# Two attention layers of a decode step on one core: second attentions paired with the next token's first, FFNs of two tokens joined, half-size load buffers

## The chip, the core and the metric

The kernel runs on one core of one Trainium2 chip. The metric is the time on the device in microseconds (us), from repeated executions; lower is better.

Names used below: PE is TensorE (matmuls; every matmul is preceded by a weight load of its own), DVE is VectorE, ACT is ScalarE, SP is the engine whose queue issues all loads. "The queue" is this load queue. A load can be issued only when its buffer is free, so the queue itself can wait for PE or DVE.

## The reference

Four tokens (batch 4, one position each) go through attention, FFN, attention, FFN, and both layers use the same weights and the same caches.

```python
B, Sq, D = 4, 1, 448
Hq, Hkv, Sk, Dh = 16, 8, 8192, 256          # F = 1792 in the FFN
W = min(4096, max(256, Sk // 4))            # = 2048: only the last 2048 positions are attended

x = A_x
x = x + A(layernorm(x))     # q = x @ wq; softmax(q k^T / 16) v; @ wo
x = x + F(layernorm(x))     # (silu(x @ w_gate) * (x @ w_up)) @ w_down
x = x + A(layernorm(x))     # the same k_cache, v_cache, wq, wo
x = x + F(layernorm(x))
```

For one token and one of the 8 KV heads, K is 2048 x 256 bf16, which is 1 MiB, and V is 1 MiB too. That unit of work, (token, layer, KV head), is called a *pair* below; there are 4 x 2 x 8 = 64 of them. A *first* attention is layer 0, a *second* attention is layer 1. A second attention needs the same K and V as the first; what was kept on the chip isn't loaded again.

## The kernel before

Operations are put into a graph; a list scheduler with assumed durations fixes the order on each engine, and waits are placed after that. So on each engine the order is static: an operation that is ready waits behind one that is not. The parts that the change touches:

```python
NK = 2; NKT = 5; NV = 6            # raw K buffers, transposed K, V buffers: 1 MiB each
KEEP_KT = 4; KEEP_V = 4; FILL = 4  # heads kept from the first attention for the second

def pair_sequence():
    # ... one(t): 8 first pairs of token t; two(t): 8 second pairs, the kept heads first
    return (a + b[:FILL] + a2 + b[FILL:] + c[:FILL] + b2 + c[FILL:] + d[:FILL]
            + c2[:HKV - FILL] + d[FILL:] + c2[HKV - FILL:] + d2)
...
# all weights first: wq, then wo head by head, and the FFN's weights at rank 7.2
for nm, wsb, src in (("wg", wg_sb, B_w_gate), ("wu", wu_sb, B_w_up)):
    load(7.2, 3 * 458752, ...)
...
for pos, (t, layer, kvh) in enumerate(seq):
    # K: one load of 1 MiB into Kr, then two DVE transposes into KT          (L520, L526)
    # V: one load of 1 MiB into Vs                                           (L533)
    # scores: 32 matmuls, KT is the weight operand, q moves 8 columns        (L541)
    # max over positions by two matmuls M, exp on ACT, sums and a permutation on PE
    # p.V: 32 matmuls, V is the weight operand, p moves 2 columns            (L589)
    # out projection: 16 matmuls, wo is the weight operand, 1 column         (L608)
    ...
    def out_proj(e, p_=p_, t=t, kvh=kvh):
        for cc in range(4):
            for k in range(4):
                last = e.matmul(Ab[:, 4 * t + cc:4 * t + cc + 1], lhsT=wo_sb[:, 4 * kvh + k, c0:c0 + 128],
                                rhs=oT[p_][:, k // 2, k % 2:k % 2 + 1], ...)
    ...
    if all 8 heads of (t, layer) are done:       # written out in the kernel
        after_attention(t, pos)                  # residual, norm, ffn of this token alone: 168 matmuls
        if layer == 0: norm(t, pos); qproj([t], pos)
        else: store(t, pos)
```

## Time and profile before

| | before |
|---|---|
| median of the first three runs, us | 406.53 (403.88 to 406.92) |
| span of the profiled execution, us | 401.2 |
| loaded, MB | 112.83 |
| PE busy, us | 255.0 (64%) |
| DVE busy, us | 204.6 (51%) |

Lines of the profile page of the kernel before: the span, the busy time of each engine, then rows of 40 equal slices of the span (each digit is the busy share in tenths, GB/s is what the loads moved in a slice), the load queue's line of the queue table (packets, MB, share), and the chain of waits that ended last, by engine.

```profile
span 401.2 us, 16386 instructions
PE 255.0 (64%) x7572; PEld 231.9 (58%) x7572; DVE 204.6 (51%) x642; ACT 59.5 (15%) x302; POOL 2.7 (1%) x11
PE   2255005667777657877676766676776776677965
DMA  7999999968983999759839999379939969617200
GB/s 302 407 387 383 398 402 402 402 230 270 381 301 116 382 402 395 289 182 343 321 107 309 397 396 373 108 221 377 311 99 384 389 226 344 227 66 218 103 3 2
q1 hardware_dynamic: 39968, 112.83, 76.2%
PE 37%; DMA 19%; DVE 18%; SPq 12%; issue 10%; ACT 3%; DVEq 0%
```

No engine is full, and the loads aren't either: the DMA row swings between 9 and 3. The fifth and sixth digit of the PE row are 0: there PE waits for the first K, whose load stands behind the FFN's weights.

The table of windows of the kernel before: stretch, its length, busy time and instructions of each engine, granted clock, share of the DMA engines, GB/s.

```profile
core 0: us, PE busy (x) PEld busy (x) DVE busy (x) ACT busy (x) POOL busy (x), PEclk, DMA share, GB/s
50.00:80.00 30.00, 11.63 (x324) 10.12 (x324) 12.77 (x24) 2.60 (x14) 0.00 (x0) 1.00 1.04 403
100.00:355.00 255.00, 180.49 (x5524) 165.49 (x5521) 137.00 (x416) 40.21 (x212) 0.00 (x0) 1.00 0.80 293
335.80:375.90 40.10, 30.27 (x939) 28.09 (x940) 17.82 (x69) 5.57 (x28) 0.00 (x0) 1.00 0.59 207
375.90:401.20 25.30, 16.76 (x508) 15.24 (x505) 7.04 (x36) 3.08 (x18) 0.00 (x0) 1.00 0.01 3
```

The first line shows what the loads can do (403 GB/s), the second what they did (293).

The queue's waits in the kernel before (which load waited for which operation: total us, times, longest):

```profile
SPq L520 <- DVE KT L526: 92.0, 16, 10.2
SPq L533 <- PE Y L589: 51.6, 19, 7.5
SPq L520 <- DVE rs L578: 37.2, 6, 10.7
SPq L533 <- PE M L554: 32.5, 13, 5.1
```

L520 is the K load and L533 the V load. So loads stop because buffers are held: K waits for the transposes, V for the matmuls that read it.

### The profile page before, as it was taken

The numbers are of one execution on the slowest core, as the hardware profiler recorded it, in microseconds if no ns is written. First come the engines' busy times: TensorE is split into PE (matmuls) and PEld (weight loads), VectorE is DVE, ScalarE is ACT, GpSimd is POOL, SyncE is SP. The second block draws the span as 40 slices with busy tenths as digits, with TensorE's granted clock in tenths as the row PEclk, the third lists the DMA queues.
The fourth block names the chain that finished last, engine by engine and source line by source line (L and its number), as shares of the span: only waits on it lengthen the run. The fifth ranks groups of instructions, "written<-read, shape, count | busy, mean of one in ns | idle before, by whom it ended". The sixth has DMA issues, their size and how long they took to land.

```text
span 401.2 us, 16386 instructions
## 1 busy us (share of the span) xinstructions
PE 255.0 (64%) x7572; PEld 231.9 (58%) x7572; DVE 204.6 (51%) x642; ACT 59.5 (15%) x302; POOL 2.7 (1%) x11
## 2 busy tenths in 40 slices
PE   2255005667777657877676766676776776677965
PEld 2254004556676656766575665566765666667855
DVE  6721005688526635487336465286365665345432
ACT  1024001111012112111111111011121120111210
POOL 2000000000000000000000000000000000000000
DMA  7999999968983999759839999379939969617200
GB/s 302 407 387 383 398 402 402 402 230 270 381 301 116 382 402 395 289 182 343 321 107 309 397 396 373 108 221 377 311 99 384 389 226 344 227 66 218 103 3 2
DMA packets 40036, 113.88 MB, mean 284 GB/s; under 512 B 1816, under 2 KB 7968, under 8 KB 33440
## 3 DMA queue, kind: packets, MB, share of 16 engines
q1 hardware_dynamic: 39968, 112.83, 76.2%
q8 instruction: 59, 0.97, 1.0%
q14 instruction: 9, 0.07, 0.0%
HBM read 112.82 MB, written 0.00 MB: 281 GB/s over the span
## 4 chain that ended last, share of the span: by engine, by line
PE 37%; DMA 19%; DVE 18%; SPq 12%; issue 10%; ACT 3%; DVEq 0%
DMA Kr<-in_A_k_cache_dram 19%; DVE KT L526 11%; SPq L312 8%; PE Y L589 8%; PE S L541 7%; PE Z L437 6%; PE A L608 5%; PE Z L399 4%; SPq L533 3%; PE Z L456 3%; ACT oT L598 2%; PE Z L342 1%; ACT qb L421 1%; DVE negm L557 1%; PE Z L344 1%
## 5 line engine op out<-in xcount | busy, mean ns | idle before, releaser
L526 DVE STREAM_TRANSPOSE KT<-Kr 128x1024 uint32<-128x1024 uint32 x96 | 117.1, 1230 | 45.2 <-DMA Kr<-in_A_k_cache_dram 44.9
L541 PE MATMUL S<-qb,KT 128*128 128x8 bf16 x2048 | 63.8, 168 | 40.9 <-DVE KT L526 30.4
L541 PEld LDWEIGHTS S<-qb,KT 128*128 128x128 bf16 x2048 | 60.3, 104 | 44.8 <-DVE KT L526 31.9
L589 PE MATMUL Y<-pT,V 128*128 128x2 bf16 x2048 | 64.3, 165 | 22.4 <-issue 13.0
L589 PEld LDWEIGHTS Y<-pT,V 128*128 128x128 bf16 x2048 | 60.5, 104 | 24.4 <-issue 15.5
L608 PE MATMUL A<-oT,wo_sb 128*128 128x1 bf16 x1024 | 37.7, 166 | 18.8 <-ACT oT L598 10.5
L608 PEld LDWEIGHTS A<-oT,wo_sb 128*128 128x128 bf16 x1024 | 33.7, 105 | 25.7 <-ACT oT L598 16.9
L598 ACT ACTIVATE oT<-Y,rinv 128x2 bf16<-128x2 f32 x128 | 26.5, 258 | 104.7 <-PE Y L589 43.5
L547 DVE TENSOR_REDUCE pmax<-S 128x2 bf16<-128x32 f32 x64 | 11.7, 183 | 51.0 <-PE S L541 47.6
L557 DVE TENSOR_REDUCE negm<-M 128x2 bf16<-128x256 f32 x64 | 26.2, 410 | 17.9 <-PE M L554 16.2
L566 ACT ACTIVATE praw<-S 128x32 bf16<-128x32 f32 x64 | 12.6, 196 | 114.3 <-PE S L562 114.3
L437 PE MATMUL Z<-xn,wg_sb 128*128 128x1 bf16 x336 | 24.2, 165 | 2.4 <-DVE xe L381 1.7
L437 PE MATMUL Z<-xn,wu_sb 128*128 128x1 bf16 x336 | 24.0, 165 | 1.5 <-issue 1.5
L554 PE MATMUL M<-identb,pmax 128*128 128x128 bf16 x64 | 20.1, 314 | 3.1 <-issue 3.1
L552 PE MATMUL M<-identb,pmax 128*128 128x128 bf16 x64 | 17.6, 275 | 6.8 <-DVE pmax L547 6.8
L437 PEld LDWEIGHTS Z<-xn,wg_sb 128*128 128x128 bf16 x336 | 17.7, 104 | 4.5 <-issue 2.4
L562 PE MATMUL S<-negm,identb 128*128 128x32 bf16 x64 | 12.4, 193 | 11.7 <-DVE negm L557 8.1
L437 PE MATMUL Z<-xe,wu_sb 128*128 128x1 bf16 x112 | 18.5, 165 | 1.5 <-issue 1.5
L437 PEld LDWEIGHTS Z<-xn,wu_sb 128*128 128x128 bf16 x336 | 17.7, 104 | 1.6 <-issue 1.6
L437 PE MATMUL Z<-xe,wg_sb 128*128 128x1 bf16 x112 | 18.5, 165 | 0.0
L578 DVE TENSOR_REDUCE rs<-Y 128x2 f32<-128x32 f32 x64 | 11.4, 178 | 13.6 <-PE P L573 10.4
L399 PE MATMUL Z<-xn,wq_sb 128*128 128x1 bf16 (+1 forms) x480 | 17.8, 165 | 0.8 <-DVE xe L381 0.8
(70 smaller groups left out, 302.6 us busy)
## 6 DMA issues: line engine op xcount, KB each, us to landing
Kr<-in_A_k_cache_dram SPq DMA_DIRECT2D x48, 1024.0 KB, 7.8
V<-in_A_v_cache_dram SPq DMA_DIRECT2D x48, 1024.0 KB, 9.0
wo_sb<-in_A_wo_dram SPq DMA_DIRECT2D x8, 448.0 KB, 12.2
wq_sb<-in_A_wq_dram SPq DMA_DIRECT2D x3, 1024.0 KB, 7.1
wd_sb<-in_B_w_down_dram SPq DMA_DIRECT2D x1, 1568.0 KB, 14.9
wg_sb<-in_B_w_gate_dram SPq DMA_DIRECT2D x1, 1344.0 KB, 11.7
wu_sb<-in_B_w_up_dram SPq DMA_DIRECT2D x1, 1344.0 KB, 11.8
wq_sb<-in_A_wq_dram SPq DMA_DIRECT2D x1, 512.0 KB, 9.9
```

Source lines behind the costliest of these rows:

```text
L312: return e.dma_start(dst, src)
L399: last = e.matmul(o, lhsT=lhsT, rhs=rhs, start=(hh == 0 and ee == 0 and cc == 0), stop=(hh == 15 and ee == 1 and cc == 3), skip_group_chec ...
L437: last = e.matmul(Zb[:, 32 * gi + fc:32 * gi + fc + 1], lhsT=lhsT, rhs=rhs, start=(n == 0), stop=(n == 111), skip_group_check=True)
L526: return e.transpose(dst[:, 2 * hf:2 * hf + 2], src[:, 2 * hf:2 * hf + 2])
L541: last = e.matmul(Sb[p_][:, 8 * gg:8 * gg + 8], lhsT=kt[:, gg, ce // 2, ce % 2, :], rhs=qb[t][:, kvh, ce, :, :], start=(gg == 0 and ce == ...
L552: e.matmul(Mb[:, 0:128], lhsT=pmax[p_][:, 0:1].broadcast_to([128, 128]), rhs=identb[:, :], start=True, stop=False, skip_group_check=True)
L554: return e.matmul(Mb[:, 128:256], lhsT=pmax[p_][:, 1:2].broadcast_to([128, 128]), rhs=identb[:, :], start=False, stop=True, skip_group_che ...
L557: g.op(DVE, 0.4, pos, lambda e, p_=p_: e.tensor_reduce(negm[p_][:, :], Mb[:, 0:256].rearrange("p (n k) -> p n k", n=2), AX.X, ALU.max, neg ...
L566: g.op(SCA, 0.35, pos, lambda e, p_=p_: e.activation(praw[p_][:, :], Sb[p_][:, 0:32], ACT.Exp, scale=1.0 / 16.0), r=(f"s{p_}",), w=(f"praw ...
L589: last = e.matmul(Yb[p_][:, 2 * dh:2 * dh + 2], lhsT=Vs[vs][:, a, gg, 128 * dh:128 * dh + 128], rhs=pT[p_][:, k, :], start=False, stop=(dh ...
L598: last = e.activation(oT[p_][:, n, :], Yb[p_][:, 0:4].rearrange("p (d n) -> p n d", n=2)[:, n, :], ACT.Copy, scale=rinv[p_][:, n:n + 1])
L608: last = e.matmul(Ab[:, 4 * t + cc:4 * t + cc + 1], lhsT=wo_sb[:, 4 * kvh + k, c0:c0 + 128], rhs=oT[p_][:, k // 2, k % 2:k % 2 + 1], start ...
```

## The change

The intent is to keep the loads going. First and second attentions need the same compute but 16 MB and 8 to 9 MB of loads; run in blocks they alternately starve PE and stop the queue. After the change a *step* runs one second attention of a token beside one first attention of the next token, on the same KV head, so that the two share one output projection (the wo weights are loaded into PE once, two columns move). FFNs of two tokens that fall together are joined in the same way. Buffers are halves of 512 KiB (four for raw K, ten for V), so they come free sooner. That is one MiB less for V than before, and there is one transposed K buffer more. The FFN's weights are loaded after the first K and V. Norms, the maximum and the expansion of q were made leaner too; the scaling of p.V moved from ACT to DVE, and a pair's score matmuls stand earlier in the order. The core of the diff, cut:

```diff
-NK = 2
-NKT = 5
-NV = 6
-KEEP_KT = 4
-KEEP_V = 4
-FILL = 4
+NKT = 6
+NRAW = 4
+NVH = 10
+KEEP_K = 4
+KEEP_V = 3
+SHIFT = 4
+FFW = 9
 ...
+def steps():
+    first, second = orders()
+    out = [((0, 0, h),) for h in first[0]]
+    for t in range(1, B):
+        for i, h in enumerate(first[t]):
+            if i >= SHIFT:
+                out.append(((t - 1, 1, h), (t, 0, h)))
+            elif t > 1:
+                out.append(((t - 2, 1, h), (t, 0, h)))
+            else:
+                out.append(((t, 0, h),))
+    out += [((B - 2, 1, h),) for h in second[B - 2][HKV - SHIFT:]]
+    return out + [((B - 1, 1, h),) for h in second[B - 1]]
 ...
-        Kr = [sb(f"Kr{s}", [128, 16 * DH], BF16) for s in range(NK)]
-        Vs = [sb(f"V{s}", [128, 4, 4, DH], BF16) for s in range(NV)]
+        Kr = [sb(f"Kr{s}", [128, 8 * DH], BF16) for s in range(NRAW)]
+        Vh = [sb(f"V{s}", [128, 2, 4, DH], BF16) for s in range(NVH)]
 ...
+            assert n == 1 or pairs[0][0] < pairs[1][0]
-                        last = e.matmul(Ab[:, 4 * t + cc:4 * t + cc + 1], lhsT=wo_sb[:, 4 * kvh + k, c0:c0 + 128],
-                                        rhs=oT[p_][:, k // 2, k % 2:k % 2 + 1], start=False, stop=False,
+                        last = e.matmul(Av[:, cc, sl], lhsT=wo_sb[:, 4 * kvh + k, c0:c0 + 128],
+                                        rhs=oT[si % 2][:, k // 2, k % 2, 0:n], start=False, stop=False,
 ...
+        for si, pairs in enumerate(steps()):
+            if si == FFW:
+                g._dep(ffn_head, last_load[0], False)     # FFN weights only after this K load
 ...
+                if layer == 0:
+                    with_ = [t - 2] if t >= 2 else []
+                    ffn(with_ + [t], pos)
 ...
+                elif t == B - 1:
+                    ffn([t - 1, t], pos)
+                    store([t - 1, t], pos)
```

## The prediction

> **What bounds it now.** 112.8 MB (queue table) in a span of 401.2 us: 284 GB/s. Unhindered, the queue moves 403 GB/s (table of windows, 50 to 80 us); from 100 to 355 us only 293. Loads alone would need 280 us. No engine is full: in that stretch PE is busy 71%, DVE 54%. The queue's own waits: K loads for transposes 92.0 us and for later DVE work about 90, V loads for PE about 110. Chain of waits: PE 37%, DMA 19%, DVE 18%, queue 12%, "issue" 10%. A first attention loads 16 MB, a second 8 for the same compute; they run in blocks, the DMA row swings between 9 and 3, and buffers for two transfers can't bridge a block. The last 26 us move nothing: pairs at 2.9 us each, norm, FFN, store.
>
> **What changes.**
> - DMA: V kept for 3 heads, not 4: 104 half loads for 48 whole, +4.2 MB. K bytes unchanged. 117.0 MB, an estimate of 290 us at 403 GB/s.
> - PE: output projections 1024 to 704 matmuls, FFN 1344 to 840, M 128 to 64. At 27 ns each in a dense run (32 in 0.85 us) an estimate of 22 us, plus some 10 from M and the norm's f32 matmuls.
> - DVE: transposes stay (96 x 1.23 us). negm halves its input (0.41 us, an estimate of 0.28). Added: oT from ACT, about 12 us, and eight qb masks. Sum about equal, 205 to 215 us.
> - Order: a step pairs a second attention with the next token's first, so loads per compute even out: four steps of 4 MB (10.4 us of DMA), four of 2.1 to 2.6 MB (about 5.9 us); two pairs cost PE about 5 us. FFN weights come after the first K and V, so the 24 us wait for K at 35 to 59 us goes.
> - Halves free Kr and V sooner; bytes in flight stay the same. An issue took the queue 0.34 to 0.38 us unblocked, so 200 are affordable.
>
> **On the critical path.** The chain should become DMA; PE savings matter only in the light steps and the tail. Per token: 65 us of DMA; PE about 50 us plus 6 to 9 of "issue" gaps (38 us in all now, up to 3.1 each). The Trainium skill (Runtime: NRT & Kernel Launch, Instruction fetch mechanics) calls crossing an instruction block "mostly hidden"; here gaps of about 2.6 us show, so I keep them. Near balance, so I allow some 5 us of loss per token. Sum: 2.5 start + 290 + 18 tail without loads + 15 losses = 326 span, 328 measured.
>
> **Predicted: 328 us; 8 in 10 between 313 and 348.** Faster by over 2%: 0.96; within 2%: 0.03; slower: 0.01.
>
> **Right if** the mean rises to 350 to 375 GB/s, the DMA row is 9 almost to the end, the largest waits on DVE and PE are for Kr and V, the queue's waits shrink below 120 us though issues double, PE busy is near 220 us. **Wrong if** the row still swings (static orders on PE and DVE block a ready softmax behind a late transpose), if halves lower the unblocked rate below 390, or if ten V halves, six held, make V wait for PE in the 4 MB steps: then 345 to 365. If the tail hides under the last loads: 315. The Trainium skill (HBM Reference, Specifications) gives about 425 GB/s for a core alone; the trace sustains 403, which I use.

## The result

| | before | after |
|---|---|---|
| median, us (4 runs each) | 406.73 (403.88 to 408.43) | 349.45 (349.34 to 349.99) |
| span of the profiled execution, us | 401.2 | 347.6 |

The ratio is 0.860 (95% interval 0.855 to 0.865): the change is faster by 14%. The four runs of the kernel before lie within 1.2% of each other. A ratio is the mean time of one kernel's fast runs over that of the other's of the same rounds, so not quite the ratio of the medians. Executions over 1.5% slower than the fastest of the same kernel are left out of the means. The forecast of 328 us was 21 us too low, and the result lies 1.5 us above the range's upper end of 348.

The page of the changed kernel, the same lines, with one more of the queue table (q8 brings instructions, not data):

```profile
span 347.6 us, 14580 instructions
PE 220.3 (63%) x6648; PEld 199.3 (57%) x6648; DVE 201.2 (58%) x759; ACT 26.5 (8%) x145; POOL 0.8 (0%) x7
PE   3452245366666477588567666858568584698875
DMA  7999999999989999999999998999999999763700
GB/s 281 399 392 391 393 395 395 392 403 393 399 279 385 395 397 356 309 378 386 389 389 397 390 381 316 312 393 318 386 397 394 396 337 400 254 234 125 243 4 2
q1 hardware_dynamic: 49824, 117.04, 90.7%
q8 instruction: 52, 0.85, 1.0%
DMA 37%; PE 36%; issue 13%; DVE 10%; ACT 1%; SPq 1%; ACTq 0%
```

The DMA row is now 9, twice 8, from the second slice to about 295 us, where it thins out to 7, 6, 3, 7 before it ends. "SPq" in the chain fell from 12% to 1%, and "issue" rose to 13%.

The table of windows of the changed kernel, its columns as before:

```profile
20.00:80.00 60.00, 27.54 (x776) 24.12 (x777) 28.82 (x79) 3.55 (x18) 0.00 (x0) 1.00 1.05 395
79.00:291.10 212.10, 144.41 (x4468) 131.42 (x4466) 133.35 (x465) 16.41 (x97) 0.00 (x0) 1.00 1.00 370
291.10:328.40 37.30, 29.03 (x904) 26.54 (x902) 19.81 (x98) 3.24 (x18) 0.00 (x0) 1.00 0.71 246
328.40:347.60 19.20, 13.00 (x403) 11.89 (x399) 6.24 (x39) 1.21 (x7) 0.00 (x0) 1.00 0.01 3
```

These windows are cut at events: 79.0, 148.5, 218.9 and 291.1 us are the starts of the FFNs that follow the first attention of the four tokens, 328.4 us is the landing of the last K or V load. So 79.0 to 291.1 is the steady part, three tokens of 69.5, 70.4 and 72.2 us (mean 70.7).

The queue's waits of the changed kernel (L587 loads K, L601 loads V); lines for other loads and smaller ones are left out:

```profile
SPq L601 <- PE Y L646: 64.5, 37, 6.0
...
SPq L587 <- DVE KT L593: 23.9, 15, 4.1
SPq L587 <- DVE st L416: 22.9, 9, 10.2
SPq L601 <- PE M L617: 19.3, 16, 3.9
```

The wait of K for transposes fell from 92.0 to 23.9 us. The K and V lines add up to some 290 us before and 212 us after.

Where the 53.6 us of span came from, by the starts of the FFNs in the two traces:

| stretch | before, us | after, us | gain, us |
|---|---|---|---|
| start to the first FFN | 100.7 | 79.0 | 21.7 |
| first FFN to the last token's layer-0 FFN | 235.1 | 212.1 | 23.0 |
| from there to the end | 65.4 | 56.5 | 8.9 |

### The profile page after: what moved, and what is told of

It reads as the page before. It is cut to its first block, busy times and chain, and to the rows that moved or that the text cites. A ratio compares the mean times of both kernels' runs of the same rounds, so it can differ in the third digit from the quotient of the medians.

```text
span 347.6 us, 14580 instructions
## 1 busy us (share of the span) xinstructions
PE 220.3 (63%) x6648; PEld 199.3 (57%) x6648; DVE 201.2 (58%) x759; ACT 26.5 (8%) x145; POOL 0.8 (0%) x7
## 3 DMA queue, kind: packets, MB, share of 16 engines
q1 hardware_dynamic: 49824, 117.04, 90.7%
## 4 chain that ended last, share of the span: by engine, by line
DMA 37%; PE 36%; issue 13%; DVE 10%; ACT 1%; SPq 1%; ACTq 0%
DMA Kr<-in_A_k_cache_dram 23%; DMA V<-in_A_v_cache_dram 15%; PE Y L646 11%; PE S L609 10%; DVE KT L593 6%; PE Z L490 4%; PE A L680 3%; PE Z L445 3%; PE Z L517 2%; DVE qb L470 1%; ACT pT L635 1%; SPq L346 1%; DVE oT L655 1%; PE Z L386 1%; ACT praw L627 1%
## 5 line engine op out<-in xcount | busy, mean ns | idle before, releaser
L593 DVE STREAM_TRANSPOSE KT<-Kr 128x1024 uint32<-128x1024 uint32 x96 | 117.7, 1230 | 31.0 <-DMA Kr<-in_A_k_cache_dram 30.8
L609 PEld LDWEIGHTS S<-qb,KT 128*128 128x128 bf16 x2048 | 60.1, 104 | 45.8 <-DVE KT L593 22.6
L614 DVE TRANSPOSE_TENSOR_REDUCE pmax<-S 128x1 bf16<-128x32 f32 x64 | 13.4, 209 | 34.5 <-PE S L609 23.0
L680 PE MATMUL A<-oT,wo_sb 128*128 128x1 bf16 (+1 forms) x704 | 26.0, 166 | 7.6 <-issue 4.2
L635 ACT ACTIVATE pT<-P 128x32 bf16<-128x32 f32 x64 | 12.6, 197 | 151.0 <-PE S L623 94.3
L617 PE MATMUL M<-identb,pmax 128*128 128x128 bf16 x64 | 17.5, 273 | 7.2 <-DVE pmax L614 6.0
L445 PEld LDWEIGHTS Z<-xn,wq_sb 128*128 128x128 bf16 x480 | 17.5, 104 | 5.8 <-DMA wq_sb<-in_A_wq_dram 4.3
L620 DVE TENSOR_REDUCE negm<-M 128x2 bf16<-128x128 f32 x64 | 18.0, 282 | 2.6 <-PE M L617 1.2
L445 PE MATMUL Z<-xe,wq_sb 128*128 128x1 bf16 (+1 forms) x160 | 17.5, 165 | 0.0
L445 PEld LDWEIGHTS Z<-xe,wq_sb 128*128 128x128 bf16 x160 | 16.6, 104 | 0.6 <-issue 0.6
L632 PE MATMUL Y<-praw,onesb 128*128 128x32 bf16 x64 | 12.0, 188 | 2.1 <-issue 2.1
L629 PE MATMUL P<-praw,permb 128*128 128x32 bf16 x64 | 12.2, 191 | 0.7 <-ACT praw L627 0.7
## 6 DMA issues: line engine op xcount, KB each, us to landing
wu_sb<-in_B_w_up_dram SPq DMA_DIRECT2D x1, 1344.0 KB, 15.2
```

Of the source, the lines that this page charges most:

```text
L445: last = e.matmul(o, lhsT=lhsT, rhs=rhs, start=(hh == 0 and ee == 0 and cc == 0), stop=(hh == 15 and ee == 1 and cc == 3), skip_group_chec ...
L593: return e.transpose(dst[:, 2 * hf:2 * hf + 2], src)
L609: last = e.matmul(Sb[p_][:, 8 * gg:8 * gg + 8], lhsT=kt[:, gg, ce // 2, ce % 2, :], rhs=qb[t][:, kvh, ce, :, :], start=(gg == 0 and ce == ...
L614: g.op(DVE, 0.18, pos, lambda e: e.tensor_reduce(pmax[p_][:, :], Sb[p_][:, 0:32], AX.X, ALU.max, apply_transpose=True), r=(f"s{p_}",), w=( ...
L617: g.op(PE, 0.18, pos, lambda e: e.matmul(Mb[:, 0:128], lhsT=pmax[p_][:, 0:1].broadcast_to([128, 128]), rhs=identb[:, :], start=True, stop= ...
L620: g.op(DVE, 0.28, pos, lambda e: e.tensor_reduce(negm[p_][:, :], Mb[:, 0:128].rearrange("p (k n) -> p n k", n=2), AX.X, ALU.max, negate=True),
```

## The question, and the theories

The gain is large but 22 us of span short of the forecast. Two lines of the profile looked like an explanation: "issue" in the chain of waits, and PE's waits. The first four of the changed kernel's PE waits, largest first (wait, releaser: total us, times, longest):

```profile
PE S L609 <- DVE KT L593: 21.5, 8, 10.3
PE Y L646 <- issue: 14.2, 10, 3.9
PE S L609 <- issue: 11.4, 7, 2.5
PE Y L646 <- DMA V<-in_A_v_cache_dram: 10.5, 13, 2.3
```

All waits of PE that are called "issue" together are 42.9 us. One of them in the timeline of PE in the changed kernel (start, us, line, operation, count, idle before):

```profile
267.57 1.16 PE L646 MATMUL Y<-pT,V 128*128 128x2 bf16 x32
268.59 0.99 PE L609 MATMUL S<-qb,KT 128*128 128x8 bf16 x32
269.45 0.24 PE L680 MATMUL A<-oT,wo_sb 128*128 128x2 bf16 x4
271.46 0.48 PE L680 MATMUL A<-oT,wo_sb 128*128 128x2 bf16 x12 [1.77 <-issue]
```

The gap falls in the middle of 16 matmuls that all had their data. I counted PE's instructions in the trace (a matmul with its weight load is two) and set them against the packets of the instruction queue q8, of 16 KiB each. A packet is then a block of 256 instructions. One number was fitted, at which instruction the first border lies; fitted separately, it is the same, 194, in both kernels. With it, the gaps at block borders add up to 51.3 us in the changed kernel and 44.6 us in the kernel before, where at an arbitrary position they come to 2 us (the median over all 256 positions). This sum includes ordinary waits that happen to stand at a border, and it depends a little on how it is counted: a second count from the same traces gave 50.8 and 46.1 us, so differences of 2 us in it mean nothing. My count of the blocks, changed kernel, in us (blocks 39 and 42 are left out; their waits were 2.29 and 2.84 us):

```
block  PE enters  fetch of next   wait for  fetch   last instr.  first of    gap
       it         block starts    start     ends    of block     next block
 36     259.37     262.73          3.36     263.83    264.43      265.11     0.69
 37     265.11     268.94          3.83     270.07    269.50      271.45     1.95
 38     271.45     275.20          3.75     276.30    275.75      277.57     1.83
 40     282.40     286.54          4.14     287.42    286.10      288.79     2.69
 41     288.79     294.30          5.51     295.38    293.42      296.75     3.34
 43     302.11     303.24          1.12     304.32    306.26      306.29     0.03
 44     306.29     308.78          2.50      309.76    310.68      310.98     0.30
 45     310.98     312.11          1.13     313.06    316.80      316.83     0.03
```

The fetch of the next block starts only after PE has entered the present one (in 51 of the 52 blocks). While the load queue is full that start comes 1.2 to 5.9 us later (median of all blocks 3.2 us), the packet takes about 1 us, and 1.3 to 1.5 us more pass before its first instruction runs. That sums to about 6 us, while the 128 matmuls of a block take about 3.4 us if dense (27 ns each). At the fetches of blocks 43 and 45 the load queue moves little (173 and 105 GB/s in the five microseconds around them): the start comes after 1.1 us and there is no gap. At that of block 44 it moves 244 GB/s, and the values lie between. In the full part blocks follow each other every 5.98 us (mean of blocks 13 to 43).

From this come the theories that the expectations below name:

- **F (fetch).** With a full load queue, PE's program arrives at about one block in 6 us, and that sets PE's pace. Matmuls then cost about 46 ns each, not 27, and the total follows the number of blocks.
- **B (loads and buffers).** Loads and the buffers that hold them back bind; PE has slack. Added matmuls cost little, and smaller buffers or other orders change the time.
- **P (plain PE work).** PE is on the critical path but without any fetch effect; an added matmul costs its 27 ns of a dense run.
- **T (tail).** The forecast failed at the end of the kernel, after the last token's layer-0 FFN, where the order leaves too many pairs.

The experiments change the changed kernel, and their ratios are against the kernel before on the same chip, whose medians there were 405 to 408 us. "Gap sum" below is the sum of the gaps at block borders.

## The experiments

### Round 1: is it fetch, loads, or plain PE work?

**Output projections per token again.** The order stays, 320 matmuls (2.5 blocks) come back.

```diff
-                        last = e.matmul(Av[:, cc, sl], lhsT=..., rhs=oT[si % 2][:, k // 2, k % 2, 0:n], ...)
+                        for j, (tt, _, _) in enumerate(pairs):
+                            last = e.matmul(Av[:, cc, tt:tt + 1], lhsT=..., rhs=oT[si % 2][:, k // 2, k % 2, j:j + 1], ...)
```

> Three theories of what holds the changed kernel at 349 us (its own time 349.4). F, instruction fetch: PE's program comes in blocks of 16 KB (256 instructions, 128 matmuls with their weight loads); in the trace the gaps called issue stand exactly at block borders, a block's fetch starts 3.1 to 3.9 us after PE enters the block before it while loads fill the queue and 1.1 us after when the queue is empty, and from 122 to 302 us PE gets one block per 6.0 us. B, loads and buffers: the load stream and the waits for free buffers bind, the gaps cost nothing. P, PE work: matmuls cost their 27 ns, no more. This run undoes the shared output projections and nothing else (320 more matmuls, 2.5 blocks; order on every engine unchanged). F: 2.5 x 6 = about +13 to +15 us, 362 to 365 us. P: 320 x 27 ns = +8.6 us, 358 us. B: 349 to 351 us.

Measured: 363.94 us (361.21 to 365.07), ratio 0.894 (0.885 to 0.902). That is 14.5 us more than the changed kernel's median on another chip, or 45 ns per added matmul (13.7 us by the two ratios). B as stated is out: the added work was not hidden. F's number fits and P's 358 lies outside the four runs, but the gap sum rose only from 51.3 to 53.9 us, so the extra time isn't found at the borders.

**Small loads.** After the first filling of each buffer, a load brings 1/8 of its bytes. The result is wrong (the buffers hold old data; the comparison with the reference passed all the same, so its tolerance doesn't see it). Instructions are the same, and the load queue is nearly empty.

```diff
+                    kn = 2048 if (first load of this buffer) else 256
-                        Kr[kr][:, :], ksrc[:, 2048 * hf:2048 * hf + 2048]), ...
+                        Kr[kr][:, 0:kn], ksrc[:, 2048 * hf:2048 * hf + kn]), ...
-                        Vh[v][:, :, :, :], vsrc[:, 2 * hv:2 * hv + 2, :, :]), ...
+                        Vh[v][:, 0:va, 0:vn, :], vsrc[:, 2 * hv:2 * hv + va, 0:vn, :]), ...   # va, vn = 1 after the first
```

> Wrong results on purpose. After the first load of each K and V buffer, later loads into it bring 1/8 of their bytes; order and waits on every engine unchanged. So this is the time of everything but the load stream. F: the gaps at block borders shrink, since a fetch no longer stands behind loads: PE gets a block per about 4.3 us in the stretch that takes 6.0 now, and the whole takes 225 to 255 us. If the gaps have nothing to do with the loads: the stretch of 30 blocks keeps most of its 180 us and the tail its 46, the whole takes 275 us or more. B would also expect a clear gain, but with gaps of the same size per block.

Measured: 280.74 us (two runs, 280.45 and 281.03), ratio 0.691. The gap sum fell to 5.9 us, the median wait for the fetch's start to 0.57 us, the block period to 4.39 us, and PE's waits called "issue" from 42.9 to 2.4 us. The table of windows of this run, from its first FFN to its last token's layer-0 FFN, and from there to the end:

```profile
69.60:228.60 159.00, 138.10 (x4470) 128.66 (x4467) 130.43 (x466) 16.31 (x97) 0.00 (x0) 1.00 0.25 70
228.60:278.70 50.10, 41.49 (x1300) 38.09 (x1296) 26.00 (x136) 4.46 (x25) 0.00 (x0) 1.00 0.09 23
```

The same instructions take 53.0 us a token, and the part from the last layer-0 FFN on takes 50.1 us with almost no loads, against 56.5. So F is right about what makes the gaps. Its total was missed, and lies where the other view expected it (275 us or more), for two reasons: until the first FFN at 69.6 us many loads were still full ones, and the tail hardly shrank. Most of the tail is made neither by loads nor by gaps.

**Three and four loads in flight.** From the 21st large load on, a load waits until the one three (four) before it has landed. A shorter queue should let the fetch in earlier.

```diff
         g.schedule()
+        loads = [o for o in g.order[SP] if o.nbytes >= 1 << 18]
+        for i in range(20, len(loads)):
+            loads[i].waits.append(loads[i - 3])      # 4 in the other kernel
```

> From the 21st load on, each load is issued only when the one three before it has landed (an added wait on the queue, nothing else changed): at most 1.5 MB in flight, where up to 4 MB are now. F: the fetch waits fall from 3.1 to 3.9 us to about 2, a block comes every 4.5 to 5 us while PE has work, and the time falls to 320 to 338 us, unless the queue starves between loads (then its rate where nothing else holds it falls below 380 GB/s, and the first 120 us grow). B and P: an added wait can only cost: 350 to 370 us.

> The same with four in flight (2 MB), in case three starve the queue. F: fetch waits about 2.5 to 3 us, 330 to 345 us. B and P: 349 to 355 us.

Measured: three in flight 415.48 us (412.9 to 416.63), ratio 1.022; four in flight 362.96 us with one slow run of 370.48 (fast runs 359.33 to 364.54, ratio 0.891); for four, both forecasts were missed. F's was wrong in direction. The fetch did start sooner (medians 2.1 and 2.8 us instead of 3.2) and the gap sums fell to 11.6 and 20.0 us, but the loads starved. The table of windows of the run with three:

```profile
100.00:380.00 280.00, 156.26 (x4831) 142.65 (x4831) 144.45 (x509) 17.36 (x103) 0.00 (x0) 1.00 0.88 291
```

That is 291 GB/s, where the changed kernel has 370 in its steady part; PE's largest waits are now those for V (57.1 us) and for transposed K (33.1 us), no longer the gaps. The profiled execution with four in flight was the slow one, so its 2.8 and 20.0 us only go along with what the fast one with three shows. Here fewer gaps were worth nothing, because they cost load rate.

### Round 2: FFNs apart, the order of before, other matmuls, five in flight

**FFNs of one token at a time.** 504 matmuls (3.9 blocks) come back; the order shifts a little.

```diff
-                    ffn(with_ + [t], pos)
+                    for u in with_:
+                        ffn([u], pos)
+                    ffn([t], pos)
...
-                    ffn([t - 1, t], pos)
+                    ffn([t - 1], pos)
+                    ffn([t], pos)
```

> Undoes the joining of the FFNs alone: 504 more matmuls (3.9 blocks of PE program), the two FFNs of a step one behind the other; the schedule shifts with it. F: 3.9 blocks at 6 us where the queue is full and about 4.5 in the tail = +19 to +23 us, 368 to 373 us. P: 504 x 27 ns = +13.6 us, 363 us. B: less than +5 us.

Measured: 369.88 us (366.34 to 370.76), ratio 0.913: 20.4 us more, 40 ns per matmul. The total again fits F better than P's 363, and again the border gaps don't rise with it (46.1 us). So both runs say that PE work costs more than its dense time, about 40 to 45 ns, and neither proves that the fetch is why.

**The order of before.** Single pairs in the sequence of before, no shared projections, no joined FFNs; halves, late FFN weights and lean norms stay.

```diff
+    # steps(): its body replaced by
+    return [(p,) for p in pair_sequence()]       # the sequence of before
...
-                    with_ = [t - 2] if t >= 2 else []
+                    with_ = []
```

> The changed kernel with the order of before: a second attention in blocks, one pair to a step, so nothing to share or join (824 more matmuls, 6.4 blocks), but half-size buffers, new norm, later FFN weights, three V kept. If the order makes the gain: 385 to 405 us, of which 6.4 blocks x about 5 = 32 us are program to be fetched and the rest loads that stand still while a second attention runs. If the other parts make it: 345 to 370 us.

Measured: 379.73 us (376.45 to 380.61), ratio 0.937, between the two forecasts. So of the 57 us, about 30 belong to order, sharing and joining together, and 27 to the rest (FFN weights after the first K and V, halves, norms, and the smaller parts of the diff).

**V as the moving operand.** In p.V the two columns of p become the weights and 256 columns of V move, for all steps but the last eight: 16 matmuls and two to turn the result in place of 32, in all 784 matmuls fewer (6 blocks).

```diff
+                        last = e.matmul(Yb[p_][0:2, 64:64 + DH], lhsT=pT[p_][:, 4 * gg + 2 * hv + a, :],
+                                        rhs=Vh[vs[hv]][:, a, gg, :], ...)
+                        # then an ACT copy to ov and two matmuls with the identity that turn it
```

> Up to the last eight pairs, V is the moving operand of its products and the probabilities the weights: 16 matmuls of 256 columns and two small ones to turn the result, where there were 32 of 2 columns. PE's arrays work longer (16 x about 0.12 us = 1.9 us for 0.86, an estimate from the 0.06 us between two 128-column products in the trace; +1.1 us a pair, 56 pairs, +60 us in all), but 14 of some 95 matmuls a pair go, 784 in all, 6.1 blocks. F: fewer blocks win where the queue is full: 335 to 347 us. P: more PE work loses: 355 to 400 us. B: about 349 us, or slower by the longer chain of a pair.

Measured: 376.69 us (374.4 to 378.35), ratio 0.931, so 27 us slower than the changed kernel. F's forecast fell, and the result lies in P's range. The gap sum is only 7.0 us, but the page of this run shows what was paid (PE's busy line, and the rows of PE and of the granted clock in tenths of full speed):

```profile
PE 309.0 (83%) x5864; PEld 233.6 (63%) x5864; DVE 207.6 (56%) x759; ACT 44.2 (12%) x201; POOL 0.8 (0%) x7
PE   3474468697799999699979999889889998998975
PEclk9998587685559999955955899855969999755555
```

The array works 309 us in place of 220 (141 us of it in these matmuls, 319 ns each in the mean), and the granted clock fell to a mean of 0.756 (0.744 to 0.756 in the four runs). Because PE's work and its clock changed along with the blocks, the run doesn't tell what fewer blocks alone would be worth.

**Five in flight.** The same limit as above with 5.

> Five loads in flight (2.6 MB), after three gave 415 us (rate 282 GB/s, gaps at block borders 16 us in all) and four 363 us (317 GB/s, 20 us in all). Under F fetch waits and the load rate pull against each other; at five the rate should be nearly whole and the gaps 30 to 45 us: 345 to 354 us. B and P: 349 to 352 us. So this run looks for the best depth more than it tells theories apart.

Measured: 348.12 us (347.5 to 349.24), ratio 0.861 (0.855 to 0.868): the same as the changed kernel. The gap sum is 45.0 us. (The expectation's 16 us of gaps for three in flight come from another count than the 11.6 us above.) Of three, four and five, only five keeps the load rate (372 GB/s from its first FFN to the last token's layer-0 FFN, where the changed kernel has 370), and it leaves the fetch nearly where it was (median wait 3.1 us).

### Round 3: the tail, and the halves

**A shift of 2 and of 3 in place of 4.** With a smaller shift, a second attention starts fewer steps after its token's first, and fewer pairs of the third token are left for the end.

```diff
-SHIFT = 4
+SHIFT = 2        # 3 in the other kernel
```

> T, the tail theory: what the forecast missed is mainly the time after the last token's first attention. From its FFN to the end the changed kernel takes 56.5 us, and 50.1 us with loads cut to 1/8, so this stretch is compute and block fetches, not loads. A second attention here starts two steps after its token's first instead of four, so ten pairs and not twelve are left for that stretch; bytes, kept buffers and instructions hardly change (one dual step more). T: two pairs of about 4.4 us less, 338 to 343 us, if the chain FFN, norm, queries (16 to 19 us) fits in two heavy steps (21 us of loads); if it doesn't, each token waits a few us and the time is 345 to 355. If the tail waited for loads or for buffers: 349 us.

> The same with three steps: one pair less in the tail, and more slack for the chain. T: 343 to 346 us. If the tail waited for loads or buffers: 349 us.

Measured: shift 2, 362.01 us (361.79 to 362.1), ratio 0.890; shift 3, 356.39 us (355.75 to 357.03), ratio 0.876. Both lie above every time that was named. From the last token's layer-0 FFN to the end they take 57.1 and 57.0 us, against 56.5. T as stated, "fewer pairs left, shorter tail", is wrong. My reading is that the pairs of the other token fill waits inside the last token's own chain, and that taking them away leaves the chain as long: FFN, norm, q, eight second pairs, FFN, one after the other. A smaller shift also takes slack from the steady part: shift 2 has tokens of 73.5, 78.9 and 71.5 us.

**Whole loads.** The changed kernel with 1 MiB loads into two raw K and five V buffers.

```diff
-NRAW = 4
-NVH = 10
+NRAW = 2
+NVH = 5
```

> K and V come in loads of 1 MB into whole buffers again (2 for raw K, 5 for V, the same bytes of buffer), all else as changed. If halves matter because they free memory sooner: 355 to 375 us. If the fetch of PE's program sets the pace (F), the finer loads matter less: 350 to 358 us, with gaps at block borders of 40 to 55 us as now.

Measured: 355.46 us (355.02 to 357.08), ratio 0.874. So halves are worth 6.0 us. The time lies in both forecasts, so it doesn't tell them apart. Halves cost nothing much in rate: from 20 to 80 us the whole loads ran at 398 GB/s, halves at 395, the kernel before at 396.

### Round 4: can the order be made for the real pace?

The scheduler assumes 34 ns per matmul. With 46 ns, it would order as if it knew F.

```diff
-        MM = 0.034
+        MM = 0.046
```

> The static order of every engine is made with 34 ns for a matmul; the trace of the changed kernel gives 46 to 48 from 122 to 302 us (a block of 128 per 6.0 us). This run makes the order with 46 ns; the same instructions, buffers and loads. If part of what is lost per token (70.7 us where loads alone are 66) comes from an order that expects a faster PE: 340 to 347 us. If the block fetch itself is the loss, whatever the order: 348 to 353 us.

> The same order with five loads in flight at most, which alone gave 348.1 us and gaps at block borders of 45 us for 51. If the two add: 338 to 346 us; if order does nothing: about 348 us.

Measured: 353.99 us (353.0 to 358.0), ratio 0.876, and with five in flight as well 355.51 us (354.37 to 356.93), ratio 0.877. Both are slower than the changed kernel and than either forecast. Yet the gap sum of the first is only 31 us, and PE's waits called "issue" are 22.6 us for 42.9: fewer gaps in the steady part did not shorten the kernel. The part from the last layer-0 FFN on took 52.1 us in the first, 4.4 less than in the changed kernel (55.4 in the second), while the tokens before it took longer (72.7, 74.4, 72.5 us).

So the cost was raised for the end alone: from step 28, from step 28 with five in flight, and from step 32 with five in flight.

```diff
         for si, pairs in enumerate(steps()):
+            if si == 28:          # 32 in the last kernel
+                MM = 0.046
```

> With 46 ns for a matmul in making the order, the tail (last FFN of a first layer to the end) took 52.1 us for 56.5, but a token took 72.4 to 74.4 us for 70.7. This run makes the order with 34 ns up to step 27 and with 46 ns from step 28 on, the last token's first attention. If the tail's length is in part its order: tail near 52 us, tokens near 70.7, 343 to 347 us. If the shorter tail was luck of the longer tokens before it: 348 us or more.

> The same with at most five loads in flight from the 21st load on, which alone gave 348.1 us. If the small gains add: 342 to 346 us.

> The same, but 46 ns only from step 32 on (after the last token's first attention), five in flight. If only the tail's own order counts: as the run before, 342 to 346 us.

Measured: 350.57 us (349.58 to 351.92), ratio 0.874 (0.863 to 0.884); 347.96 us (fast runs 345.81, 346.1 and 349.82, a slow one 354.9), ratio of fast runs 0.865; 345.78 us (343.88 to 348.25), ratio 0.862 (0.852 to 0.872). On that chip the kernel before scattered from 399 to 412 us, and only three of its seven runs count as fast, so these intervals are wide. The last kernel's median is 3.7 us below the changed kernel's, its ratio isn't below it. No version is shown to beat the changed kernel. The first lies where "luck" was forecast (348 us or more): with 46 ns from step 28 the token before the tail took 76.1 and 74.3 us in the first two of these runs (72.2 in the changed kernel).

The part from the last layer-0 FFN on took 54.8, 55.5 and 54.4 us. The chains of waits say what these differences are. The table takes the pieces called "issue" out of the chain in this last part of each profiled execution, in us:

| kernel | last part | "issue" in its chain | the rest |
|---|---|---|---|
| changed | 56.5 | 7.3 | 49.2 |
| small loads | 50.1 | 1.4 | 48.7 |
| five in flight | 56.0 | 7.0 | 49.0 |
| shift 2, shift 3 | 57.1, 57.0 | 8.5, 7.5 | 48.6, 49.4 |
| 46 ns, and with five in flight | 52.1, 55.4 | 2.2, 5.5 | 49.9, 49.9 |
| 46 ns from step 28, and with five in flight | 54.8, 55.5 | 4.7, 5.4 | 50.1, 50.1 |
| 46 ns from step 32, five in flight | 54.4 | 3.6 | 50.8 |

In all of these no load stands in that part of the chain. (It does in two others: with whole loads 6.2 us of 58.7, with the projections per token 3.8 of 58.6.) The rest stays at 49 to 51 us; what varies is mostly the gaps. So the shorter tail of the run with 46 ns is fewer gaps rather than less work on the path.

## Why the prediction was right or wrong

The sum of the prediction, term by term. "Loss" is the time of a stretch less what its bytes take at 395 GB/s.

| term | predicted, us | measured, us | how |
|---|---|---|---|
| start | 2.5 | 2.5 | taken over |
| loads at full rate | 290 | 296.3 | 117.04 MB at 395 GB/s, the rate from 20 to 80 us |
| losses | 15 | 15.2 | 291.1 less 2.5, less 107.98 MB at 395 GB/s |
| losses after the last token's layer-0 FFN | not in the sum | 14.4 | 9.06 MB in 37.3 us, 22.9 at 395 GB/s |
| tail without loads | 18 | 19.2 | 328.4 to 347.6 us |
| span | 326 | 347.6 | |

**The step that failed is the sum "290 + 18 tail without loads + 15 losses": it lets the loads set the pace to their last byte, and the allowance of "some 5 us of loss per token" covers three tokens only.** For the three tokens of the steady part the allowance was right: 70.7 us a token, of which 26.2 MB at 395 GB/s are 66.3, so 4.4 us of loss. Some of that is luck: 15 was allowed and not worked out, and with the prediction's own 403 GB/s the same stretch has 20.7 us of loss. But the allowance stopped at 291 us as if the loads ended there. 9 MB were still to come, and they did not run at full rate: 246 GB/s until 328 us. The queue's waits in that stretch show why, first in the list of the changed kernel from 291 to 328 us:

```profile
SPq L601 <- PE Y L646: 14.2, 5, 6.0
```

V buffers come free only as the pairs of the end run. The loads that are left follow the last token's serial chain, not the other way round. The small-loads run shows it: with almost no loads, and gaps gone, the stretch to the end still takes 50.1 of its 56.5 us. So does the chain of waits: in these 56.5 us it holds 7.3 us of "issue", 49.2 us of work and waits on the engines, and no load. The prediction's terms for the same part, 9 MB at 403 GB/s and 18 us, come to 40.5 us. And it could be read before: the windows of the kernel before have 40.1 us at 207 GB/s ahead of the 25.3 us without loads, and I had read only the latter. The missing term is 14.4 us, two thirds of the error of 22 us. The prediction's own remark on this stretch, that the tail might hide under the last loads, had it the wrong way round.

**The second error is the rate,** 6.3 us. 403 GB/s was read from 30 favourable microseconds. In the same stretch of 20 to 80 us before had 396 GB/s and after has 395, and whole loads had 398. So the halves did not lower it, which the prediction named as a risk; the reading was too good.

**The tail without loads** was predicted at 18 us and took 19.2: right.

**The start.** The wait for K from 35 to 59 us went, as said, and the first FFN starts 21.7 us earlier. Neither the order nor the halves made this: the first FFN starts at 79.6 us in the run with the order of before and at 79.5 with whole loads, for 79.0 here. What is left is mainly the later FFN weights and the leaner norms. That it is the weights is argued from the wait for K that went, not isolated.

**The order.** Evened-out loads did what was intended until about 295 us. The DMA row is 9 (twice 8) to there, not "almost to the end", and the mean is 339 GB/s, not 350 to 375, because of the same last stretch (to 291.1 us it is 374). The digits hide some loss: slices that show a 9 have as little as 309 GB/s in the row below.

**The gaps called "issue".** The prediction kept 6 to 9 us of them per token. PE's waits called "issue" are 7.4, 15.0 and 14.7 us in the three tokens of the steady part, so about twice as much in two of them. The net loss per token still came out right, since much of the idle time of PE lies under loads. What makes the gaps is shown: the block fetch starts late behind a full load queue. What they cost is shown for the end alone: there they are 7.3 us of the chain, and the small-loads run, with 1.4, is 6.4 us shorter. In the steady part it is not shown. An upper bound comes from what a token takes: 70.7 us, of which loads alone need 66.3; and the run with 46 ns, whose order differs too, had far fewer gaps at no gain. The small-loads run can't split these 4.4 us, because it removes loads and fetch delay together, and shortening the queue starves the loads before it frees the fetch. Added matmuls cost 40 to 45 ns rather than 27, which agrees with F, but not at the borders where F would put it; this stays open.

**PE and DVE.** PE busy near 220 us: 220.3. DVE 205 to 215: 201.2, just below. The reduced maximum was estimated at 0.28 us, and it is 0.282. The largest wait of DVE is for Kr, 30.8 us, as said; that of PE is for KT and the gaps, not for V.

**The queue's waits** were to fall below 120 us and are 212. A queue that is ahead of its buffers waits often and need lose nothing by it: 64.5 us of it is V waiting for p.V, 37 times for 1.7 us in the mean, while the steady part moves 370 GB/s. This was a bad sign to choose: a queue's waits say little unless the rate falls with them.

**What the gain is made of.** Order, sharing and joining together about 30 us; the rest 27. The run with the order of before tells where: its first FFN starts at 79.6 us (before 100.7, after 79.0), and from there to the last token's layer-0 FFN it takes 235.5 us (before 235.1, after 212.1). So the gain at the start belongs to the rest, and the gain of the middle to order, sharing and joining. Halves are worth 6.0 us in the changed order; how much of the 27 they are was not measured. Sharing projections alone is worth 14.5 us and joining FFNs 20.4, each taken out alone. Their sum of 35 is more than the 30 for all three, so they overlap with the order and can't be added.

## What to carry to other kernels

When summing a forecast, cut the trace at the last point where the queue runs full, not at the last load: what comes between is a serial chain with loads trickling behind it, and it has to be measured as a chain. Take an unhindered rate over the longest clean stretch there is, in the same stretch of both kernels. And when the chain shows "issue", look whether the gaps stand at block borders, and where they lie: here they cost time in the serial chain at the end, while in the steady part under full loads no run showed that removing them helps. Added matmuls cost 40 to 45 ns here and not their dense 27, so a dense run is a poor price for them; why is open.

## What the Trainium skill lacked or had wrong

- "Runtime: NRT & Kernel Launch", section "Instruction fetch mechanics": the blocks of 16 KiB with 256 instructions agree (52 packets of 16 KiB for PE's program here, borders at the same instruction in both kernels). That crossing a border is "mostly hidden" does not hold behind a full load queue: gaps at borders add up to 51.3 us of a span of 347.6, and to 44.6 of 401.2 in the kernel before. With small loads they are 5.9 us.
- The same section gives PE a larger instruction memory than the other engines, 128 KiB, and also says that it holds two lines only. In the changed kernel's trace the fetch of a block starts only after PE has entered the block before it, in 51 of 52 blocks, so no more than one block is ahead, which fits two lines.
- "Trainium Kernel Development and Optimization", Key Constraints: it says that DMAs issued from SP, ACT and POOL run on the same 16 engines and interleave. Here SP alone issues, so no run shows it for these three. No page gives a figure for how late an instruction packet starts behind loads: here it starts 0.57 us (median) after PE enters a block with small loads, and with full loads 3.2 us in the median of all blocks and up to 5.9 us.
- "HBM Reference", Specifications: about 425 GB/s for a core that streams alone. The best stretch of these runs had 403, the long ones 395 to 398.
- "TensorE: Matmul & The Clock Gate", Part 1: it tells of a clock that is low when PE is idle and rises with activity. With V as the moving operand the granted clock fell to a mean of 0.756 while PE was busy 83% of the span; all other profiled executions had 1.00, with PE busy up to 77%. So a busier PE had the lower clock here. The page has further cases of a low clock, which were not tested against this run; the cause stays open.
- No page has a rule for how many loads must be in flight. With loads of 512 KiB, three gave 291 GB/s (100 to 380 us), and five gave 372 in the steady part, as many as without a limit (370).
